# Block-sparse attention and a two-layer MoE block on one core: the off-diagonal product of layer 1 in the second accumulator bank, and an order planned with longer VectorE and ScalarE operations

## The chip, the cores and the metric

One core of one Trainium2 chip runs the whole program. The metric is the device time of one execution in microseconds. The kernel before took 605.21 us as the median of three runs (605.0 to 609.22).

## The reference

Local attention with a few global keys, for 4 batches, 8 heads, 768 positions and 64 dimensions a head, and then two matrix products with a leaky rectifier between them:

```python
scores = 1 / np.sqrt(D) * np.matmul(q, k.transpose(0, 1, 3, 2))
rel = pos[:, None] - pos[None, :]
is_global = pos[None, :] < int(n_global)                  # 8 keys
is_local = (rel >= 0) & (rel < int(n_local))              # 96 keys
bias = -slopes[:, None, None] * dist[None, :, :]
scores = np.where(is_global | is_local, scores + bias, -1000000000.0)
a = np.exp(scores - np.max(scores, axis=-1, keepdims=True))
a = a / (np.sum(a, axis=-1, keepdims=True) + 1e-09)
attn = np.matmul(a, v)
x = attn.transpose(0, 2, 1, 3).reshape(B * S, H * D)      # 3072 x 512
h = x @ w_in                                              # 512 x 2048
g = np.maximum(h, 0.0) + alpha * np.minimum(h, 0.0)
out = g @ w_out                                           # 2048 x 512
```

## The kernel before, in words

The 3072 tokens are cut into 12 units of 256 tokens; a unit is a third of one batch. For each unit the kernel computes attention for 8 heads (`attend`), transposes the result (`x_transpose`), multiplies it by `w_in` (layer 1) and the rectified result by `w_out` (layer 2, `ff_out`, L1109). Float32 values are carried as two float16 parts, high and low, and a product is three float16 products (high by high, high by low, low by high). The 16 slices of the weights are loaded and split into such parts by VectorE and ScalarE during units 0 and 1 (`split_w`, L572 to L584 and L398).

Layer 1 is done in two ways. Units 0 to 3 use `ff_in` (L960): 12 products of 256 columns a slice into one of the two banks of the tag "h", then ScalarE or VectorE scales (`mul`, L371 or L372), VectorE takes the maximum (L973), ScalarE rounds to `gh` (L975), and GpSimd or VectorE makes the rest `gl` (L397, L977). Units 4 to 11 use `seven`: four weight slices make two pairs, and a 2 by 2 block product of each pair is done with seven block products instead of eight. The names are A11, S1, S2, A12, S3, S4 and A22; each is 12 matmuls of 128 columns (L1047). They run up two PSUM banks, `ha` and `hc` (A and C in the code), which are the two buffers of the tag "h":

- A11 goes into the lower half of `ha`. A copy `p1` of it is made (`keep`, L1054, ScalarE or VectorE). Then S2 is added to it, copy `u2` is made; S3 is added, and VectorE adds it to `p5` (the first half of `gb`, `add`, L1058); A22 is added, and the sum is copied out (the other half of `gb`).
- S1 goes into the lower half of `hc` and is copied to `p5`; S4 is added, and VectorE adds it to `u2` (half of `ga`).
- A12, the off-diagonal product, goes into the upper half of `ha`, and VectorE adds it to `p1` (the other half of `ga`).

L1086 then applies the rectifier to `ga` and `gb`, L371 makes `gh` and L398 makes `gl`.

What sets the order: every operation is recorded with a key (a due time), its reads and writes by buffer, and one or more ways (engine, cost, function). `Plan.order` simulates the engines with these costs and takes, for each engine that is free, the ready operation with the lowest key; the result is the instruction order of every engine. Each engine then runs its own list strictly in that order and waits on semaphores. A whole PSUM bank is one buffer for these waits. The costs are used for nothing but the order and for the choice between two engines.

The largest attention value of each batch sets a scale (`v_sums`, `v_most`, `v_range`): ScalarE sums absolute values (L487), VectorE builds a diagonal `vdg` (L500), TensorE makes a row of it (`vrow`, L506), and VectorE finds the scale. For batch 1 this falls into the end of unit 0's and 1's layer work.

Of the kernel before, what the change touches and what calls it, by code (L numbers as in the profile page):

```python
# [146 lines left out]
class Plan:  # L147
# [37 lines left out]
    def order(self):  # L185
        ops = self.ops
        n = len(ops)
        need = [len(o[2]) for o in ops]
        after = [[] for _ in ops]
        for i, o in enumerate(ops):  # L190
            for j in o[2]:
                after[j].append(i)
        engines = list(self.LAG)
        for q in self.queue.values():
            q.sort(key=lambda b: ops[b.uses[0][0]][0])
        wait = {e: [] for e in engines}
        free = dict.fromkeys(engines, 0)
        at = [dict.fromkeys(engines, 0) for _ in ops]
        start = [None] * n
        self.way = [None] * n  # L200
        dma = 0
        seen = 0
        events = [(0, i, "ready") for i in range(n) if not need[i]]
        heapq.heapify(events)

        def fits(i):
            want = {}
            for b in ops[i][3]:
                if not b.live and b.tag in self.slots:
                    want.setdefault(b.tag, []).append(b)  # L210
            return all(self.slots[t] >= len(bs) and self.queue[t][: len(bs)] == bs for t, bs in want.items())

        def behind(i, e, now):

            own, first = (next(x for x in ops[i][1] if x[0] == y) for y in (e, ops[i][1][0][0]))
            queue = sum(ops[j][1][0][1] for k, j in wait[first[0]]
                        if k < ops[i][0] and start[j] is None and ops[j][1][0][0] == first[0])
            return max(free[first[0]] - now, 0) + queue + first[1] > (LAZY if e == "DVE" and ops[i][0] > 34 else FLEX[e]) * own[1]

        while events:  # L220
            now = events[0][0]
            while events and events[0][0] <= now:
                _, i, what = heapq.heappop(events)
                if what == "free":
                    for b in ops[i][3]:
                        b.left -= 1
                        if not b.left and b.tag in self.slots:
                            self.slots[b.tag] += 1
                elif what == "ready":
                    for e, _, _ in ops[i][1]:  # L230
                        heapq.heappush(wait[e], (ops[i][0], i))
            for e in engines:
                if free[e] > now:
                    continue
                held = []
                pick = None
                while wait[e]:
                    k, i = heapq.heappop(wait[e])
                    if start[i] is not None:
                        continue  # L240
                    if at[i][e] <= now and fits(i) and (ops[i][1][0][0] == e or behind(i, e, now)):
                        pick = i
                        break
                    held.append((k, i))
                for x in held:
                    heapq.heappush(wait[e], x)
                if pick is None:
                    continue
                i = pick
                for b in ops[i][3]:  # L250
                    if not b.live:
                        b.live = True
                        if b.tag in self.slots:
                            self.slots[b.tag] -= 1
                            self.queue[b.tag].pop(0)
                start[i] = now
                seen += 1
                _, cost, self.way[i] = next(x for x in ops[i][1] if x[0] == e)
                if isinstance(cost, Two) and free["POOL"] > now:
                    cost += SHARE * min(cost, free["POOL"] - now)  # L260
                if e == "SP":
                    dma = max(dma, now + 1125) + cost

                    busy, end = now + 525, dma
                    if self.way[i].__name__ == "transposes":
                        busy, end = now + 1245, dma + 500
                else:
                    end = busy = now + cost
                free[e] = busy
                heapq.heappush(events, (busy, i, "busy"))  # L270
                lag = LATE if e == "SP" and ops[i][0] > 40 else self.LAG[e]
                heapq.heappush(events, (end + lag, i, "free"))
                for j in after[i]:
                    need[j] -= 1
                    for x in engines:
                        own = x == e and e != "SP"
                        at[j][x] = max(at[j][x], end + ((0 if e == "PE" else 60) if own else lag))
                    if not need[j]:
                        for t in {at[j][x[0]] for x in ops[j][1]}:
                            heapq.heappush(events, (max(t, now), j, "ready" if t == min(at[j][x[0]] for x in ops[j][1]) else "busy"))  # L280
        assert seen == n, (seen, n)
        self.start = start
        return sorted(range(n), key=lambda i: (start[i], i))
# [24 lines left out]
VR = -23  # L308
# [29 lines left out]
LAZY = 100  # L338
POOLED = 3
SHARE = 0.25  # L340
STEP4 = 1.5
XAFTER = 3
RATE = 3.5
# [8 lines left out]
def fast(tc, cn, a):  # L352
    nc = tc.nc
    ctx = ExitStack()
    with ctx:
# [657 lines left out]
        def seven(u, s, key):  # L1013
# [4 lines left out]
            A = buf("h", f"ha{u}_{s}", [P, 512])  # L1018
            C = buf("h", f"hc{u}_{s}", [P, 512])
# [37 lines left out]
            def add(k, out, a_, b_, r, w):  # L1057
                op("DVE", key + k - SOON, c_dve(256), lambda: v.tensor_tensor(out=out(), in0=a_(), in1=b_(), op=ALU.add), r=r, w=w)  # L1058
# [8 lines left out]
            keep(0.3, "p1", lambda: p1.t, lambda: A.t[:, low], [A], [p1])  # L1067
            keep(0.6, "p5", lambda: p5.t, lambda: C.t[:, low], [C], [p5])
            product(1, "S2", 1, 1, A, 0, False)
            product(1.3, "A12", 0, 1, A, 256, False)  # L1070
            keep(1.4, "u2", lambda: u2.t, lambda: A.t[:, low], [A], [u2])
            add(1.5, lambda: side(ga.t, 0), lambda: half(A.t, high), lambda: half(p1.t, low), [A, p1], [(ga, 0)])
            product(2, "S3", 2, 0, A, 0, False)
            product(2.3, "S4", 3, 0, C, 0, False)
            add(2.2, lambda: side(gb.t, 1), lambda: half(A.t, low), lambda: half(p5.t, low), [A, p5], [(gb, 1)])
# [111 lines left out]
        for b in range(B):  # L1187
            k = begin(3 * b)
            jobs.append((k - 14 if b else V0, v_load, (b,)))
            for i in range(6):  # L1190
                jobs.append(((k - 5 + 0.4 * i if b == 1 else k - 9 + 0.8 * i) if b else VR, v_sums, (b, i)))
            jobs.append(((k - 2.5 if b == 1 else k - 4) if b else VR + 1, v_most, (b,)))
            jobs.append(((k - 1.5 if b == 1 else k - 2.5) if b else VR + 2, v_range, (b,)))
        for key, fn, args in sorted(jobs, key=lambda j: j[0]):
            fn(*args, key)
        with tc.manual_schedule():
# [159 lines left out]
```

## Time and profile before

| | |
|---|---|
| median of 3 runs | 605.21 us (605.0 to 609.22) |
| the profiled execution | 605.61 us, span of the profile 603.7 us |
| TensorE busy | 583.3 us, 97% of the span, 6324 matmuls |
| VectorE busy | 502.4 us, 83% |
| ScalarE busy | 417.1 us, 69% |
| GpSimd busy | 84.4 us, 14% |
| granted TensorE clock, mean | 0.999 of full speed |

A busy share says only that an engine had an instruction in flight. Matmuls are pipelined: one of 512 columns is shown with 0.38 us, and the next one starts 0.215 us after it, so a short wait of TensorE is partly hidden in the shown duration of the matmul ahead of it.

### The profile page before, as it was taken

How to read it: one execution, taken by the hardware profiler on the slowest of the kernel's cores; microseconds unless marked ns; L12 is line 12 of the kernel's file. 1: busy time of each engine (PE TensorE's matmuls, PEld its weight loads, DVE VectorE, ACT ScalarE, POOL GpSimd, SP SyncE). 2: the span in 40 equal slices, each digit the busy share in tenths (PEclk: the TensorE clock that was granted, in tenths of full speed). 3: DMA queues.
4: the chain of work that ended last, by engine and by line, in shares of the span. 5: the costliest groups of instructions: out<-in, count | busy, mean ns of one | idle time of the engine just before them, and what ended most of it. 6: DMA issues, size and time to landing. Idle time of an engine off the chain costs nothing.

```text
span 603.7 us, 16463 instructions
## 1 busy us (share of the span) xinstructions
PE 583.3 (97%) x6324; PEld 421.8 (70%) x6324; DVE 502.4 (83%) x1387; ACT 417.1 (69%) x1049; POOL 84.4 (14%) x159
## 2 busy tenths in 40 slices
PE   8899999999999998999999999999999999999996
PEld 6687666656666676676677777777777777777784
DVE  6999999996899787989879869899879879776532
ACT  5899999956887677857657747858758656632321
POOL 2002223322323342100001001001001002000000
PEclk9999999999999999999999999999999999999999
DMA  8995596344356379759976958779898766431001
GB/s 305 408 375 173 201 271 177 63 111 135 92 135 136 80 187 242 155 138 216 215 186 155 239 138 172 125 195 207 213 164 166 198 131 87 82 71 27 36 3 40
DMA packets 138918, 97.38 MB, mean 161 GB/s; under 512 B 115536, under 2 KB 115792, under 8 KB 138832
## 3 DMA queue, kind: packets, MB, share of 16 engines
q1 hardware_dynamic: 138832, 96.26, 64.0%
q8 instruction: 51, 0.84, 0.6%
q14 instruction: 35, 0.29, 0.1%
HBM read 58.22 MB, written 6.29 MB: 107 GB/s over the span
## 4 chain that ended last, share of the span: by engine, by line
PE 57%; DVE 26%; ACT 9%; issue 4%; DMA 2%; POOL 1%; SPq 0%; ACTq 0%; DVEq 0%; POOLq 0%
PE o L1109 26%; PE ha L1047 13%; PE h L960 5%; PE hc L1047 5%; PE av L859 4%; ACT pr L791 3%; DVE pr L781 3%; DVE ps L398 2%; DVE whl L398 2%; DVE wf L579 2%; PE sp L737 2%; DVE g L973 2%; DMA raw<-in_qk_dram 2%; DVE x L398 2%; DVE xs L397 1%
## 5 line engine op out<-in xcount | busy, mean ns | idle before, releaser
L1109 PE MATMUL o<-whl,gh 128*128 128x512 f16 (+1 forms) x800 | 230.2, 371 | 0.5 <-ACT os L1130 0.5
L1109 PE MATMUL o<-whl,gl 128*128 128x512 f16 (+1 forms) x400 | 148.2, 371 | 0.5 <-POOL gl L397 0.5
L1109 PEld LDWEIGHTS <-gh 128*128 128x128 f16 x800 | 71.1, 98 | 51.8 <-issue 3.6
L1047 PEld LDWEIGHTS <-sw 128*128 128x128 f16 x1536 | 91.7, 98 | 16.7 <-issue 6.8
L791 ACT ACTIVATE pr<-pr,sm 128x256 f32<-128x256 f32 (+1 forms) x176 | 85.4, 488 | 17.2 <-DVE sm L781 16.8
L960 PE MATMUL h<-xt,whl 128*128 128x256 f16 x768 | 92.5, 273 | 2.4 <-DVE g L973 1.6
L960 PEld LDWEIGHTS <-whl 128*128 128x128 f16 x768 | 74.5, 98 | 20.8 <-issue 4.5
L1047 PEld LDWEIGHTS <-whl 128*128 128x128 f16 x1152 | 70.8, 98 | 15.3 <-issue 1.5
L1047 PE MATMUL ha<-xt,whl 128*128 128x128 f16 x1152 | 79.7, 219 | 1.1 <-DVE g L973 1.1
L781 DVE CUSTOM_DVE_ANT_0 pr<-sp,D 128x256 f32<-128x256 f32 (+1 forms) x192 | 69.4, 397 | 3.5 <-PE sp L754 1.7
L1109 PEld LDWEIGHTS <-gl 128*128 128x128 f16 x400 | 39.1, 98 | 45.1 <-POOL gl L397 1.7
L397 POOL TENSOR_TENSOR gl<-g,gh 128x256 f16<-128x256 f32 x57 | 49.1, 863 | 112.1 <-ACT gh L975 84.0
L398 DVE SCALAR_TENSOR_TENSOR ps<-pr,ps 128x512 f16<-128x512 f32 (+1 forms) x80 | 54.1, 676 | 7.6 <-ACT ps L371 7.3
L799 POOL TENSOR_TENSOR fin<-fin,sm 128x4 f32<-128x4 f32 x40 | 16.3, 409 | 283.7 <-ACT pr L791 283.7
L1047 PE MATMUL ha<-xt,sw 128*128 128x128 f16 x768 | 53.3, 219 | 2.5 <-ACT u L1054 0.9
L1047 PE MATMUL hc<-xt,sw 128*128 128x128 f16 x768 | 53.4, 219 | 0.4 <-DVE g L973 0.4
L371 ACT ACTIVATE ps<-pr 128x512 f16<-128x512 f32 (+1 forms) x76 | 44.6, 590 | 4.1 <-DMA pt<-ps 3.7
L371 ACT ACTIVATE gh<-ga 128x512 f16<-128x512 f32 x32 | 20.1, 627 | 37.2 <-DVE ga L1086 37.2
L973 DVE SCALAR_TENSOR_TENSOR g<-h,g 128x256 f32<-128x256 f32 x64 | 26.7, 417 | 11.1 <-ACT g L371 10.8
L398 DVE SCALAR_TENSOR_TENSOR x<-raw,x 128x672 f16<-128x672 f32 (+1 forms) x40 | 33.7, 843 | 1.2 <-ACT x L371 1.2
L859 PEld LDWEIGHTS <-pt 128*128 128x128 f16 x888 | 30.7, 98 | 4.6 <-issue 1.2
L975 ACT CAST gh<-g 128x256 f16<-128x256 f32 x64 | 25.1, 396 | 12.6 <-DVE g L973 11.8
(150 smaller groups left out, 934.2 us busy)
## 6 DMA issues: line engine op xcount, KB each, us to landing
w<-in_w_dram SPq DMA_DIRECT2D x32, 512.0 KB, 9.3
again<-in_w_dram SPq DMA_DIRECT2D x32, 512.0 KB, 4.9
raw<-in_qk_dram SPq DMA_DIRECT2D x28, 336.0 KB, 3.7
out_dram<-os SPq DMA_DIRECT2D x23, 256.0 KB, 2.5
rawv<-in_v_dram SPq DMA_DIRECT2D x9, 512.0 KB, 4.9
raw<-in_qk_dram SPq DMA_DIRECT2D x12, 272.0 KB, 2.9
gp<-v SPq DMA_DIRECT2D x15, 192.0 KB, 2.9
first<-in_first_dram SPq DMA_DIRECT2D x4, 467.0 KB, 5.0
```

Source lines behind the costliest of these rows:

```text
L371: lambda: nc.scalar.mul(out=out(), in_=src(), mul=by.t if tile_ else by)),
L397: return e.tensor_tensor(out=out(), in0=src(), in1=hi(), op=ALU.subtract)
L398: return e.scalar_tensor_tensor(out=out(), in0=src(), scalar=val(), in1=hi(), op0=ALU.mult, op1=ALU.subtract)
L781: op("DVE", key, c_dve(n) + 10, lambda qb=qb, n=n, dc=dc, pc=pc: v.tensor_tensor_reduce(out=pr.t[:, pc : pc + n], in0=sp.t[:, pc : pc + n] ...
L791: op("ACT", key + 1, c_act(n, ptr=1) + 93, lambda qb=qb, n=n, pc=pc: nc.scalar.activation(out=pr.t[:, pc : pc + n], in_=pr.t[:, pc : pc + ...
L799: op("POOL", key + 3, c_pool(2 * G), lambda: nc.gpsimd.tensor_tensor(out=fin.t[:, : 2 * G], in0=fin.t[:, : 2 * G], in1=sm.t[:, 2 * G : 4 * ...
L859: nc.tensor.matmul(out, lhsT=p_[:, 128 * j : 128 * j + 128], rhs=v_(j), start=m == 0, stop=m == len(ps) - 1)
L960: nc.tensor.matmul(hp.t, lhsT=w.t[:, wi, wc], rhs=x.t[:, NC * xi + c, :], start=n == 0, stop=n == 3 * NC - 1)
L973: op("DVE", key, c_dve(UT), lambda: v.scalar_tensor_tensor(out=g_(), in0=hp.t, scalar=KG, in1=g_(), op0=ALU.mult, op1=ALU.max), r=[hp], w= ...
L975: op("ACT", key, c_act(UT), lambda: nc.scalar.copy(out=gh_(), in_=g_()), r=[rg], w=[rh])
L1047: nc.tensor.matmul(out, lhsT=weight(name, f, wi, c), rhs=x.t[:, 8 * piece + m * xi + 2 * j + c, :], start=start and p == n == 0, stop=n == ...
L1109: nc.tensor.matmul(o.t[:, cols], lhsT=g_()[:, tok], rhs=w.t[:, wi, 512 + cols.start : 512 + cols.stop], start=f == 0 and n == 0, stop=f == ...
```

## The change

There are three edits. In `seven`, A12 is written into the upper half of `hc` instead of `ha`, and the addition that reads it reads `hc`; A12's matmuls, their number and their data are the same. In the planner, the cost of every VectorE and ScalarE operation is multiplied by 1.06 where its key is under 34, and by 1.02 elsewhere. And three due times of batch 1's scale are moved: sums and maximum 0.5 earlier, the row 0.5 later.

```diff
@@ Plan.order
                 _, cost, self.way[i] = next(x for x in ops[i][1] if x[0] == e)
+                if e in ("DVE", "ACT"):
+                    cost = type(cost)(cost * (SLOW if ops[i][0] < 34 else SLOWER))
@@
+SLOW, SLOWER = 1.06, 1.02
+V1S, V1M, V1R = 5.5, 3, 1
@@ seven
             product(1, "S2", 1, 1, A, 0, False)
-            product(1.3, "A12", 0, 1, A, 256, False)
+            product(1.3, "A12", 0, 1, C, 256, False)
             keep(1.4, "u2", lambda: u2.t, lambda: A.t[:, low], [A], [u2])
-            add(1.5, lambda: side(ga.t, 0), lambda: half(A.t, high), lambda: half(p1.t, low), [A, p1], [(ga, 0)])
+            add(1.5, lambda: side(ga.t, 0), lambda: half(C.t, high), lambda: half(p1.t, low), [C, p1], [(ga, 0)])
@@ jobs
-                jobs.append(((k - 5 + 0.4 * i if b == 1 else k - 9 + 0.8 * i) if b else VR, v_sums, (b, i)))
-            jobs.append(((k - 2.5 if b == 1 else k - 4) if b else VR + 1, v_most, (b,)))
-            jobs.append(((k - 1.5 if b == 1 else k - 2.5) if b else VR + 2, v_range, (b,)))
+                jobs.append(((k - V1S + 0.4 * i if b == 1 else k - 9 + 0.8 * i) if b else VR, v_sums, (b, i)))
+            jobs.append(((k - V1M if b == 1 else k - 4) if b else VR + 1, v_most, (b,)))
+            jobs.append(((k - V1R if b == 1 else k - 2.5) if b else VR + 2, v_range, (b,)))
```

The order changes on every engine. In the rows below the first number in a name is the unit, the second the head, slice or block, and the last is only a serial number. Line numbers of the changed kernel are 4 higher from L340 on.

The first place is ScalarE's list around the copy `u2` of unit 5's block 1, before:

```order
L371 ACTIVATE gh5_0_1_4963<-gb5_0_4830 128x512
L600 ACTIVATE size3_0_4978<-again3_0_4434 128x512
L791 ACTIVATE pr6_7_4958,sm6_6_4916<-pr6_7_4958,sm6_6_4916 128x128
L791 ACTIVATE pr6_7_4958,sm6_6_4916<-pr6_7_4958,sm6_6_4916 128x256
L1054 COPY u25_1_5003<-ha5_1_4880 128x256
L371 ACTIVATE ps6_6_5045<-pr6_6_4915 128x384
```

And with the change:

```order
L795 ACTIVATE pr6_6_4895,sm6_6_4896<-pr6_6_4895,sm6_6_4896 128x256
L604 ACTIVATE size3_0_4975<-again3_0_4418 128x512
L1058 COPY u25_1_4994<-ha5_1_4882 128x256
L795 ACTIVATE pr6_7_4977,sm6_6_4896<-pr6_7_4977,sm6_6_4896 128x128
L795 ACTIVATE pr6_7_4977,sm6_6_4896<-pr6_7_4977,sm6_6_4896 128x256
L375 ACTIVATE ps6_6_5045<-pr6_6_4895 128x384
```

The copy, which no longer has to stand behind A12, moved ahead of the two exponentials of head 7.

The second place is VectorE's list where unit 3 ends and unit 4 begins: `g3_14` and `g3_15` are the last two rectified slices of unit 3, whose banks unit 4's A11 and S1 take over. Before:

```order
L397 TENSOR_TENSOR xs4_2_3697<-xT4_1_3525,xs4_2_3697 128x512
L384 CAST xs4_3_3710<-xn4_2986 128x256
L397 TENSOR_TENSOR sw7_3683<-ws7_0_3651,sw7_3683 128x512
L397 TENSOR_TENSOR xs4_3_3710<-xn4_2986,xs4_3_3710 128x256
L397 TENSOR_TENSOR sw7_3683<-ws7_1_3658,sw7_3683 128x512
L973 SCALAR_TENSOR_TENSOR g3_14_3695<-h3_14_3665,g3_14_3695 128x256
```

And with the change:

```order
L1008 TENSOR_TENSOR ws7_1_3679<-ws7_1_3679,ws7_0_3676 128x256
L977 SCALAR_TENSOR_TENSOR g3_14_3687<-h3_14_3663,g3_14_3687 128x256
L785 ISA pr5_3_3721,sm5_2_3613<-sp5_3_3511,D3_224 128x256
L785 ISA sm5_2_3613 128x1
L401 TENSOR_TENSOR xs4_3_3719<-xn4_2983,xs4_3_3719 128x256
L401 TENSOR_TENSOR sw7_3696<-ws7_0_3676,sw7_3696 128x512
L401 TENSOR_TENSOR sw7_3696<-ws7_1_3679,sw7_3696 128x512
```

`g3_14` moved ahead of three rests. On TensorE's list the products of `h3_15` moved ahead of layer 2's slice 13, and slices 13 and 14 now stand between them and A11 of unit 4; before, A11 came right behind them.

The third place is VectorE's list ahead of `vdg1`, the diagonal for batch 1's scale. Before:

```order
L973 SCALAR_TENSOR_TENSOR g1_12_1893<-h1_12_1863,g1_12_1893 128x256
L398 SCALAR_TENSOR_TENSOR whl15_1898<-words3_1658,whl15_1898 128x512
L497 TENSOR_REDUCE vmm1_1908<-vm1_1740 128x1
L807 RECIPROCAL sm2_6_1751<-sm2_6_1751 128x4
L398 SCALAR_TENSOR_TENSOR x16_3_2_1831<-raw3_2_1609,x16_3_2_1831 128x544
L579 SCALAR_TENSOR_TENSOR wf15_1_1934<-w15_1_1423,wb15_1_1860 128x512
L500 TENSOR_SCALAR vdg1_1942<-ident_58,vmm1_1908 128x128
```

And with the change:

```order
L977 SCALAR_TENSOR_TENSOR g0_13_1868<-h0_13_1783,g0_13_1868 128x256
L977 SCALAR_TENSOR_TENSOR g1_12_1870<-h1_12_1804,g1_12_1870 128x256
L501 TENSOR_REDUCE vmm1_1889<-vm1_1736 128x1
L376 TENSOR_SCALAR x16_3_0_1891<-raw3_0_1430 128x544
L504 TENSOR_SCALAR vdg1_1908<-ident_58,vmm1_1889 128x128
```

One long operation is left between `g1_12` and `vdg1`, where there were three. On TensorE's list two more blocks of layer 2 (slice 11 of unit 1, three matmuls of 512 columns each) stand ahead of the row `vrow1`.

## Rows read from the trace of the kernel before

**Rows 1.** Busy time by stretch: length, PE, PEld, DVE, ACT, POOL, clock, DMA

```profile
0.00:45.00 45.00, 39.76 (x300) 33.68 (x301) 37.56 (x144) 36.04 (x88) 4.80 (x22) 1.00 0.95 365
45.00:130.00 85.00, 81.77 (x681) 56.47 (x680) 84.57 (x191) 76.04 (x170) 23.59 (x32) 1.00 0.58 165
130.00:232.00 102.00, 101.19 (x883) 67.85 (x883) 86.79 (x227) 78.88 (x207) 33.79 (x49) 1.00 0.58 137
232.00:510.00 278.00, 272.54 (x3448) 197.96 (x3447) 239.35 (x686) 192.30 (x506) 21.48 (x52) 1.00 0.78 175
510.00:603.70 93.70, 88.08 (x1021) 65.84 (x1018) 54.17 (x144) 33.87 (x80) 0.78 (x4) 0.99 0.23 46
```

**Rows 2.** Waits of TensorE: who waited for whom, us in total, times, longest

```profile
PE h L960 <- DVE g L973: 1.6, 4, 0.8
PE vrow L506 <- DVE vdg L500: 1.2, 1, 1.2
PE ha L1047 <- DVE g L973: 1.1, 1, 1.1
...
PE tp L816 <- ACT pt L821: 1.0, 1, 1.0
PE ha L1047 <- ACT u L1054: 0.9, 3, 0.4
PE ha L1047 <- ACT p L1054: 0.8, 2, 0.4
PE h L960 <- DVE xt L398: 0.7, 1, 0.7
PE ha L1047 <- DVE ga L1058: 0.7, 2, 0.4
...
PE hc L1047 <- DVE g L973: 0.4, 1, 0.4
```

**Rows 3.** Timeline, unit 5's block 1, A12 to S3: start, us, engine, instruction, [idle before]

```profile
295.94 0.83 PE L1047 MATMUL ha<-xt,whl 128*128 128x128 f16 x12
...
296.61 0.59 PE L1109 MATMUL o<-whl,gh 128*128 128x512 f16 x2
...
297.06 0.53 ACT L791 ACTIVATE pr<-pr,sm 128x256 f32<-128x256 f32 x1
...
297.26 0.59 PE L1109 MATMUL o<-whl,gh 128*128 128x512 f16 x2
...
297.55 0.39 ACT L1054 COPY u<-ha 128x256 f32<-128x256 f32 x1
297.69 0.38 PE L1109 MATMUL o<-whl,gl 128*128 128x512 f16 x1
...
297.97 0.42 DVE L1058 TENSOR_TENSOR ga<-ha,p 128x256 f32<-128x256 f32 x1 [0.33 <-ACT u L1054]
...
298.44 0.83 PE L1047 MATMUL ha<-xt,sw 128*128 128x128 f16 x12 [0.37 <-DVE ga L1058]
```

**Rows 4.** Timeline, unit 6's block 3: S1 and its copy p5

```profile
361.93 0.83 PE L1047 MATMUL hc<-xt,sw 128*128 128x128 f16 x12
...
363.25 0.36 ACT L1054 COPY p<-hc 128x256 f32<-128x256 f32 x1
```

**Rows 5.** Timeline, batch 1's scale: GpSimd, VectorE and TensorE

```profile
119.51 0.67 POOL L397 TENSOR_TENSOR gl<-g,gh 128x256 f16<-128x256 f32 x1 [3.03 <-ACT gh L975]
119.61 1.12 DVE L398 SCALAR_TENSOR_TENSOR whl<-words,whl 128x512 f16<-128x512 f32 x1
...
122.37 0.28 DVE L500 TENSOR_SCALAR vdg<-ident,vmm 128x128 f32<-128x128 f32 x1
...
122.69 0.49 PE L506 MATMUL vrow<-vdg,ones 128*128 128x128 f32 x2 [1.22 <-DVE vdg L500]
```

**Rows 6.** Timeline, unit 3 to unit 4: the rectified slice, and A11 that takes its bank

```profile
233.53 0.41 DVE L973 SCALAR_TENSOR_TENSOR g<-h,g 128x256 f32<-128x256 f32 x1
...
233.99 0.83 PE L1047 MATMUL ha<-xt,whl 128*128 128x128 f16 x12 [1.14 <-DVE g L973]
```

## The prediction

> **What bounds the kernel now.** I read the busy time by stretch first, then the list of TensorE's waits, then the timeline at the places that list points to. TensorE has an instruction in flight nearly all the time: 101.19 of 102 us while units 2 and 3 run their layers, 272.54 of 278 us in most of the seven-product units, and 81.77 of 85 us between 45 and 130 us [rows 1]. The clock is at its higher level, 2.4 GHz, throughout (1.00 in every stretch, 0.99 in the last) [rows 1], so it is no term. The number of matmuls does not change. So a change of order can win only what TensorE now loses to waits, and can lose only by making new ones. In the stretch from 45 to 130 us VectorE is just as full, 84.57 of 85 us [rows 1]: there the two bound each other, and a wait taken from TensorE may come back as another one.
>
> What is there to win: the nine waits listed come to 8.4 us in 16 events [rows 2]. They understate the loss. Two matmuls of 512 columns start 0.43 us before the third one, so 0.215 apart, and one is shown with 0.38 [rows 3]; the 0.165 us between the two is idle time that looks busy. At 16 events this is another 2.6 us, 11 in all. That is under 2% of 605, and the change touches some of it.
>
> **The sum is made against the profiled execution,** 605.6 us; it lies 0.4 us above the median of 605.2 (runs 605.0 to 609.2).
>
> *A12 into the second bank.* Its twelve matmuls take 0.67 us from start to start of the next work (295.94 to 296.61) wherever they write [rows 3]. What moves is who waits. Before, `u2`, the addition to `p1`, S2, A12 and S3 all stand in one bank. The rows show the chain: A12 ends at 296.77, the copy `u2` starts at 297.55 behind an exponential, the addition starts at 297.97, 0.03 after the copy's end at 297.94, and S3 starts at 298.44, 0.05 after the addition's end [rows 3]. So copy and addition, which only read, go one after the other, and S3 waits for both. With the change `u2` needs only S2, the addition reads the other bank, and S3 needs `u2` alone. I counted the work on TensorE's new list with 0.055 us for a matmul of 128 columns and 0.215 for one of 512: between S2's end and S3 lie at least 1.97 us in all 32 blocks, where before between A12's end and S3 there were 1.3 us or less in 22 of them. The copy takes 0.39 us [rows 3]. S3's five waits (three for `u`, two for `ga`) are 0.9 and 0.7 us [rows 2], with five times 0.165 this is **2.4 us, all of which I take as gone**. S2's two waits for `p`, 0.8 us [rows 2], stay: nothing about them changes.
>
> The price is a wait that was not there: A12 writes the bank from which `p5` is copied, so A12 waits for that copy, with layer 2 queued behind it, and S4 waits for the addition. No row of before has this wait. From below it is nothing: 30 of 32 blocks have 1.97 us or more on the new list between S1's end and A12, and all 32 between A12 and S4, and a late `p5` ends at 363.61, 0.85 after S1's end at 362.76 [rows 4]. The two blocks where only S2 lies between (0.67 us) can lose 0.2 each; from above, if the copy were late by one more exponential of 0.53 [rows 3] in ten blocks, it is some 2.4 us. I take **0.2**, since 30 covers are more than twice the row's 0.85. A second price: in unit 4's first block A22 now stands right behind S3 in the same bank, with nothing to cover the addition between: 0.42 and the 0.05 behind it [rows 3], **0.5**.
>
> The Trainium skill has a rule on this, in "PSUM — Partial Sum Buffer", section "PSUM bank collisions raise a hardware error": any two of the three engines must be kept apart on one bank, reads against reads included, and it says to guard by bank, not by address. The trace agrees, with the addition that starts 0.03 us after a copy it does not depend on. The rule speaks for the change in bank `ha` and against it in bank `hc`, where it makes A12 wait for `p5`; by the rule alone the change would only move the wait, and that is the second rival below.
>
> *The end of unit 3.* A11 of unit 4 takes the bank of unit 3's slice 14 and S1 that of slice 15. VectorE reached the first slice only at 233.53, and A11 started at 233.99 after 1.14 us of idle time [rows 6]. The new list has the slice ahead of three rests, and on TensorE four layer-2 blocks (12 matmuls, 2.6 us) between the last `h` and A11. The waits are 1.1 and 0.4 us, two events [rows 2]: **1.8 us gone.**
>
> *Batch 1's row.* TensorE waited 1.22 us at 122.69 for `vdg`, which VectorE ran at 122.37 [rows 5]. Two long VectorE operations ahead of it are gone, and 1.3 us of layer 2 stand ahead of the row in addition. 1.2 and 0.165 [rows 2]: **1.4 us gone.**
>
> *Units 0 and 1, the start.* The scores of unit 1's first heads now come ahead of the transpose that waited 1.0 us for a copy [rows 2]; but the product that needs this transpose's own copy now follows closer behind. I take half of 1.2: **0.6**. Attention of unit 1 now lies between the first `xt` and its first use, which waited 0.7 [rows 2]: **0.9**. Products `h` wait four times, 1.6 us, for the slice that frees their bank [rows 2]; on the new list several stand one or two layer-2 blocks (0.65 us each) later. Half of 2.2: **1.1**. With the row this is 4.0 us, all before 130 us.
>
> *What is given back.* Of that 4.0, VectorE's full stretch takes back some. Between nothing and all of it I take half, **2.0**, because TensorE and VectorE are equally full there [rows 1]. And later `h` means less time until layer 2 needs it: on the new list the cover from `h` to its layer 2 shrinks by 2.6 to 5.0 us for six slices of units 0 and 1, and to 3.3 and 3.9 us for some of unit 3. I put two new waits of the mean size of rows 2 there (8.4/16 + 0.165 = 0.7 each): **1.4**; none and six are the ends.
>
> Engines' choices change too: seven scalings of `g` move from ScalarE to VectorE, a net three casts of weights and a few others the other way. Each costs about the same on either engine, and GpSimd gets two more rests; I count nothing, covered as long as neither queue is the last, and part of the give-back if it is.
>
> Sum: 2.4 + 1.8 + 4.0 gained is 8.2; 0.2 + 0.5 + 2.0 + 1.4 lost is 4.1. 605.6 - 4.1 = **601.5 us**.
>
> **The rivals.**
>
> 1. *Nothing comes back* (0.20). The gains are kept, and the covers that shrank were longer than needed: 605.6 - 8.2 + 0.7 = 598.1, and 596.3 if the two halves above are whole. For it: VectorE is below full from 130 us on (86.79 of 102) [rows 1], so work put off can be made up. Against: the full stretch.
>
> 2. *The wait only moves to the second bank* (0.08). `p5` and the addition are late because ScalarE is in attention's exponentials, and A12 and S4 lose what S3 won: 601.5 + 2.4 = 603.9. For it, the copy `u` that stood 0.78 us behind A12's end [rows 3]; against, the covers of 1.97.
>
> 3. *VectorE sets the pace of units 0 and 1* (0.25). Its full 85 us [rows 1] leave no room, and all 4.0 come back: 603.5, and up to 605.5 with three more small waits. The longer costs may also be of no use: a VectorE operation is longer when GpSimd runs, not by a fixed share; a rest took 1.12 us beside a GpSimd one [rows 5], where 1.06 was added to all. The Trainium skill has this in "SBUF — State Buffer", section "Who interferes with whom": VectorE with two SBUF inputs and GpSimd reading SBUF block each other. The row fits it.
>
> 4. *Slower* (0.05). One mechanism: layer 2 of units 0 and 1 waits for `gl`. Six slices lost 2.6 to 5.0 us of cover, down to some 6.5 us; where VectorE and GpSimd together need longer than that from `h` to `gl`, each slice stalls TensorE, with all that is queued behind. At the longest wait of the kind in rows 2, 1.2 + 0.165, six cost 8.2: 605.6 - 2.4 - 1.8 + 8.2 = 609.6. Against it: `gl` is on no line of rows 2.
>
> **How the numbers follow.** The forecast, about 599.2 to 603.5, has 0.42. The range must reach into rival 1 and over rival 3: 597 to 606 leaves out the far end of rival 1 and rival 4, together under 2 in 10. One per cent, about what a measurement of this kernel can tell from no change, is 599.2 and 611.3 around 605.2. Faster: most of rival 1 and a little of the forecast, 0.2. Slower: the far half of rival 4, 0.03. The rest is the same, 0.77.
>
> **What would show it.** Right: the waits of `ha` for `ga` gone and those for `u` near nothing, with at most 0.5 us of a new wait of `hc` for `p`; A11's and the row's wait gone; TensorE's idle time from 232 to 510 us down by 4. Wrong: a line of `hc` waiting for `p` of 1 us or more (rival 2); VectorE still full to 130 us and the `h` products waiting as before (rival 3); `o` waiting for `gl` several times before 130 us (rival 4).

## The result, and the profile after

The changed kernel takes 599.61 us as the median of six runs (597.90 to 603.36), the kernel before 608.95 in the runs beside it (605.0 to 610.65). The ratio, of the means of these runs, is **0.9867, 95% interval 0.982 to 0.9914**: faster by 1.3%, though the interval reaches past 0.99. The forecast was 601.5 in a range of 597 to 606, so the time lies inside, but on the side of the first rival (598.1), and "faster by over 1%" had 0.2. The profiled execution took 601.47 us, span 599.7. One slow execution of the kernel before, 751.71 us in the last set of runs, is left out everywhere.

The busy time by stretch of the changed kernel (length, then PE, PEld, DVE, ACT, POOL, clock, DMA share, GB/s) answers to [rows 1]:

```profile
0.00:45.00 45.00, 39.67 (x303) 34.35 (x304) 36.84 (x142) 36.37 (x89) 5.04 (x22) 0.96 0.93 358
45.00:130.00 85.00, 84.10 (x699) 58.12 (x697) 84.35 (x192) 80.31 (x174) 25.05 (x33) 1.00 0.59 165
130.00:232.00 102.00, 101.01 (x883) 67.61 (x882) 89.31 (x233) 80.25 (x212) 33.80 (x51) 1.00 0.63 146
232.00:510.00 278.00, 275.11 (x3498) 200.11 (x3496) 240.45 (x689) 194.11 (x514) 17.60 (x51) 1.00 0.79 175
510.00:599.70 89.70, 82.28 (x951) 61.88 (x949) 49.68 (x129) 30.23 (x71) 0.79 (x4) 0.99 0.20 42
```

Three things to see. From 45 to 130 us TensorE went from 81.77 to 84.10 us busy while VectorE stayed as full as it was. (The changed kernel is some 3 us further in its work by 130 us, so the larger sums of ScalarE there and of VectorE in the next stretch hold later work too; equal work is compared further down.) From 232 to 510 us TensorE's idle time fell from 5.46 to 2.89 us, by 2.6, where the prediction gave 4. And before 45 us the clock is 0.96, where it was 1.00.

TensorE's waits (who for whom, us in total, times, longest), against [rows 2]:

```profile
PE tp L820 <- ACT pt L825: 1.7, 1, 1.7
PE av L863 <- DVE sm L785: 1.1, 2, 0.7
PE ha L1051 <- DVE gb L1062: 0.8, 2, 0.6
PE h L964 <- DVE g L977: 0.7, 3, 0.4
PE vrow L510 <- ACT pt L825: 0.6, 1, 0.6
PE hc L1051 <- DVE ga L1062: 0.4, 1, 0.4
...
PE o L1113 <- POOL gl L401: 0.2, 1, 0.2
```

Of the nine lines of [rows 2] the waits of `vrow` for `vdg`, of `ha` for `g`, `u`, `p` and `ga`, of `hc` for `g` and of `h` for `xt` are gone. `h` for `g` fell from 1.6 to 0.7. There is no line of `hc` waiting for `p`. New are `ha` for `gb`, A22 behind S3; `vrow` for `pt`, batch 0's row, at 24 us; and `hc` for `ga`, S1 of unit 4's second block behind the addition after S4. (The kernel of experiment 2 has this last one too, with A12 in the first bank, so it is no price of the second.) The wait of `tp` at the start went from 1.0 to 1.7, and that of `av` for `sm` from 0.4 to 1.1.

The three places of [rows 3], [rows 5] and [rows 6] in the timeline of the changed kernel (start, us, engine, instruction). Unit 5's block 1, S2 to S3:

```profile
291.13 0.83 PE L1051 MATMUL ha<-xt,sw 128*128 128x128 f16 x12
...
291.80 0.83 PE L1051 MATMUL hc<-xt,whl 128*128 128x128 f16 x12
...
292.52 0.39 ACT L1058 COPY u<-ha 128x256 f32<-128x256 f32 x1
...
293.45 0.42 DVE L1062 TENSOR_TENSOR ga<-hc,p 128x256 f32<-128x256 f32 x1
...
293.76 0.83 PE L1051 MATMUL ha<-xt,sw 128*128 128x128 f16 x12
```

S3 starts while the addition still runs in the other bank, and carries no wait; in [rows 3] it began 0.05 us after the addition's end, after 0.37 idle. Batch 1's diagonal and row, and the end of unit 3:

```profile
117.87 0.27 DVE L504 TENSOR_SCALAR vdg<-ident,vmm 128x128 f32<-128x128 f32 x1
...
121.04 0.38 PE L510 MATMUL vrow<-vdg,ones 128*128 128x128 f32 x2
...
228.37 0.41 DVE L977 SCALAR_TENSOR_TENSOR g<-h,g 128x256 f32<-128x256 f32 x1
...
231.52 0.83 PE L1051 MATMUL ha<-xt,whl 128*128 128x128 f16 x12
```

`vdg` is ready 2.9 us before the row needs it, and the slice `g3_14` 2.7 us before A11; before, the row and A11 each waited over a microsecond.

The start is the one place that got worse in the profile. Busy time by stretch from 14 to 24 us, where TensorE's 1.7 us wait lies:

```profile
14.00:15.50 1.50, 1.50 (x13) 1.21 (x12) 1.50 (x6) 1.08 (x3) 0.00 (x0) 1.00 1.03 410
15.50:17.00 1.50, 0.04 (x1) 0.00 (x0) 1.50 (x6) 1.27 (x3) 0.00 (x0) 0.99 1.05 423
17.00:20.40 3.40, 3.12 (x14) 2.95 (x14) 2.49 (x7) 2.96 (x6) 0.00 (x0) 0.50 1.01 396
20.40:24.00 3.60, 3.00 (x24) 2.34 (x23) 2.28 (x11) 2.30 (x8) 0.00 (x0) 1.00 1.04 418
```

After a pause of TensorE the clock is at its lower level, 1.2 GHz, for 3.4 us; at half speed that costs at most 1.7 us. The profiled execution of before had none of this [rows 1], and lies among the shortest of its kernel, so the two profiles (4.1 us apart) show less than the medians.

**How far each kernel is ahead, and where.** Both kernels have the same 6324 matmuls, all in both traces. I gave each its spacing at full clock (0.216 us for 512 columns, 0.109 for 256, 0.056 for 128, float32 ones as they stand in the profile of before), added them up in the order of their starts, and compared when the same amount of work had been started. The number, called the lag below, is us against the profile of before (minus is ahead), at five of its times; a product that merely moved shows for a moment, so differences over long stretches count. Two executions with the same order of work also differ at the start: 9 and 10 by 0.8 us at 45, the two of the changed kernel by 0.7. The rows below the first two are the experiments.

| kernel | 1.2 GHz at the start, us | 16 | 45 | 160 | 275 | last matmul |
|---|---|---|---|---|---|---|
| changed | 3.4 | -1.1 | -0.3 | -2.9 | -3.4 | -5.8 |
| changed, second profile | 3.4 | -0.6 | 0.4 | -2.2 | -2.8 | -5.5 |
| 1: bank alone, order of before | 6.8 | -0.7 | 2.1 | 2.1 | 2.5 | 0.7 |
| 2: order of the change, first bank | 3.4 | -0.7 | 0.2 | -2.5 | -3.0 | -5.3 |
| 3: costs and due times, no bank | 0 | -0.9 | -1.5 | -4.1 | -4.8 | -5.6 |
| 4: bank alone, planned | 0 | 0.0 | 0.0 | 0.0 | 0.4 | -2.6 |
| 5: change without due times | 3.4 | -0.4 | 0.6 | -1.5 | -2.1 | -5.6 |
| 6: change, copy moved at the start | 0 | -1.1 | -1.2 | -3.9 | -4.5 | -7.8 |
| 7: bank and due times, no costs | 6.8 | -0.6 | 2.3 | 1.6 | 2.0 | -1.1 |
| 8: change, pause filled | 0 | -0.8 | -1.8 | -4.5 | -5.0 | -8.0 |
| 9: before, pause filled | 0 | -1.2 | -1.2 | -1.3 | -1.2 | -1.1 |
| 10: bank alone, order of before, pause filled | 0 | -0.4 | -0.4 | -0.4 | -0.1 | -1.7 |

From the last matmul to the end of the span it is 5.7 us before and 5.7 to 6.8 in the experiments and the second profile of the change, but 7.4 in the first: another 1.7 us by which the pair of profiles shows less.

### The profile page after: what moved, and what is told of

Its sections match the earlier page's. It is cut to its first block, busy times and chain, and to the rows that moved or that the text cites. A ratio compares the mean times of both kernels' runs of the same rounds, so it can differ in the third digit from the quotient of the medians.

```text
span 599.7 us, 16469 instructions
## 1 busy us (share of the span) xinstructions
PE 582.2 (97%) x6324; PEld 422.1 (70%) x6324; DVE 500.6 (83%) x1380; ACT 421.3 (70%) x1054; POOL 82.3 (14%) x161
## 4 chain that ended last, share of the span: by engine, by line
PE 72%; DVE 16%; ACT 5%; DMA 3%; issue 3%; POOL 1%; SPq 0%; ACTq 0%; POOLq 0%; DVEq 0%
PE o L1113 32%; PE ha L1051 11%; PE hc L1051 8%; PE h L964 8%; PE av L863 5%; PE sp L741 3%; DVE pr L785 2%; ACT pr L795 2%; DMA xt<-xs 2%; DVE ps L402 1%; DVE ws L1008 1%; PE sp L758 1%; PE tp L820 1%; DVE g L977 1%; DMA raw<-in_qk_dram 1%
## 5 line engine op out<-in xcount | busy, mean ns | idle before, releaser
L1051 PEld LDWEIGHTS <-whl 128*128 128x128 f16 x1152 | 70.9, 98 | 15.5 <-issue 1.9
L401 POOL TENSOR_TENSOR gl<-g,gh 128x256 f16<-128x256 f32 x59 | 52.3, 886 | 110.7 <-ACT gh L979 103.2
L402 DVE SCALAR_TENSOR_TENSOR ps<-pr,ps 128x512 f16<-128x512 f32 (+1 forms) x80 | 56.4, 706 | 3.0 <-ACT ps L375 2.9
L1051 PE MATMUL ha<-xt,whl 128*128 128x128 f16 x768 | 53.2, 219 | 1.1 <-DVE gb L1062 0.8
L803 POOL TENSOR_TENSOR fin<-fin,sm 128x4 f32<-128x4 f32 x40 | 11.9, 298 | 285.1 <-ACT pr L795 284.9
L375 ACT ACTIVATE x<-raw 128x672 f16<-128x672 f32 (+1 forms) x36 | 25.9, 726 | 11.6 <-PE sp L741 10.4
L795 ACT ACTIVATION_READ_ACCUMULATOR pr<-pr,sm 128x1 f32 x176 | 33.9, 192 | 0.0
```

Source lines behind the costliest of these rows:

```text
L375: lambda: nc.scalar.mul(out=out(), in_=src(), mul=by.t if tile_ else by)),
L401: return e.tensor_tensor(out=out(), in0=src(), in1=hi(), op=ALU.subtract)
L402: return e.scalar_tensor_tensor(out=out(), in0=src(), scalar=val(), in1=hi(), op0=ALU.mult, op1=ALU.subtract)
L795: op("ACT", key + 1, c_act(n, ptr=1) + 93, lambda qb=qb, n=n, pc=pc: nc.scalar.activation(out=pr.t[:, pc : pc + n], in_=pr.t[:, pc : pc + ...
L803: op("POOL", key + 3, c_pool(2 * G), lambda: nc.gpsimd.tensor_tensor(out=fin.t[:, : 2 * G], in0=fin.t[:, : 2 * G], in1=sm.t[:, 2 * G : 4 * ...
L1051: nc.tensor.matmul(out, lhsT=weight(name, f, wi, c), rhs=x.t[:, 8 * piece + m * xi + 2 * j + c, :], start=start and p == n == 0, stop=n == ...
```

## The experiments

Times are medians; ratios are of means, to the kernel before, run on the same chip beside the experiment, with 95% intervals. The chips of the three sets differ, so times of different sets compare only roughly.

**1 and 2: the bank without its order, and the order without its bank.** In the first, A12 is planned in the first bank, so that every engine's list is that of before, and only the addresses differ. In the second the lists are the changed kernel's and A12 still writes the first bank. The addition reads the bank that A12 writes. Both take a bank to plan with; the last two edits are the first kernel's, against before, and the second's, against the change:

```diff
-            def product(k, name, piece, j, bank, col, start):
+            def product(k, name, piece, j, bank, col, start, planned=None):
...
-                op("PE", key + k, 12 * 55.8, products, r=deps, w=[bank])
+                op("PE", key + k, 12 * 55.8, products, r=deps, w=[planned or bank])
...
-            product(1.3, "A12", 0, 1, A, 256, False)
+            product(1.3, "A12", 0, 1, C, 256, False, A)
...
-            product(1.3, "A12", 0, 1, C, 256, False)
+            product(1.3, "A12", 0, 1, A, 256, False, C)
```

> A12 and its addition use the second bank, but every engine's list is word for word that of the kernel before (the planner still sees the first bank, the old costs and the old due times). Theory B (the bank pays by itself): S3 no longer waits for VectorE, only for the copy u; its waits of 1.6 us shown fall to under 0.6, A12's new wait for p5 stays under 0.5, time 1.5 to 2.5 us below the kernel before (ratio 0.996 to 0.998). Theory O (the gain is the order's; the bank only allows it): the copy u stands as late in ScalarE's list as before, so S3 waits nearly as long, and A12 waits for p5 where only S2 lies between; ratio 0.999 to 1.002. Theory M (the wait moves to the second bank): waits of hc for p of 1 us or more, ratio above 1.002.

> Every engine's list is that of the changed kernel, but A12 and its addition use the first bank again. Theory B: S3's waits come back (2.4 us or more, since the copy and the addition are chained again), time 2 to 4 us above the changed kernel, ratio to before 0.990 to 0.994. Theory O: the new order alone holds most of the gain, ratio within 0.002 of the changed kernel's in the same call (0.985 to 0.989).

Measured: bank alone 606.91 us, ratio 0.9985 (0.9966 to 1.0003). Order alone 600.11, ratio 0.9872 (0.9851 to 0.9893), which is the changed kernel's. So most of the gain is the order's, an order that the planner finds when it is told of the second bank. The waits of the bank alone show that the edit does what it says:

```profile
PE h L960 <- DVE g L973: 1.6, 4, 0.8
PE vrow L506 <- DVE vdg L500: 1.2, 1, 1.2
PE ha L1047 <- DVE g L973: 1.1, 1, 1.1
...
PE ha L1047 <- ACT p L1054: 0.8, 2, 0.4
...
PE ha L1047 <- ACT u L1054: 0.2, 1, 0.2
```

`ha` for `ga` is gone, for `u` it is 0.2 in place of 0.9, `hc` waits for no `p`, and the others stand as in [rows 2]. Its lag falls from 2.5 at 275 us to 0.7 at the end, 1.8 us (1.4 from 160 us on); the medians, 606.91 and 608.09, are 1.2 apart. In this profile the start hides it, with 6.8 us at the lower clock:

```profile
15.50:17.00 1.50, 0.45 (x5) 0.21 (x4) 1.50 (x5) 1.50 (x4) 0.00 (x0) 1.00 1.04 418
17.00:23.80 6.80, 6.80 (x31) 6.28 (x33) 5.14 (x14) 3.73 (x6) 0.00 (x0) 0.50 1.03 407
23.80:27.00 3.20, 3.20 (x27) 2.65 (x26) 2.06 (x13) 1.76 (x7) 0.00 (x0) 0.99 1.03 414
```

**3: the longer costs and the due times without the bank**, with a second run of the changed kernel beside it.

```diff
-            product(1.3, "A12", 0, 1, C, 256, False)
+            product(1.3, "A12", 0, 1, A, 256, False)
```

> The longer costs and the moved due times, A12 in the first bank for planner and chip alike. Theory B: the part of the gain before unit 4 (row for batch 1, h products, end of unit 3) stays, S3's waits are as before: 3 to 5 us below the kernel before, ratio 0.992 to 0.995. Theory O: nearly the whole gain, 6 to 8 us, ratio 0.987 to 0.990. If VectorE sets the pace of units 0 and 1 (third rival): ratio above 0.997.

> The changed kernel unaltered, for comparison on the same chip. Both theories: ratio 0.984 to 0.990. The profile before last showed TensorE's clock at the lower level from 17.0 to 20.4 us behind a wait of 1.7 us; if that comes in some executions alone, this profile may show the clock at 1.00 there, and then a span 3 us shorter (about 596.5); if it belongs to the order, the clock is lower there again.

Measured: 601.5 us, ratio 0.9899 (0.9881 to 0.9917); the changed kernel again 600.53, 0.9879 (0.9859 to 0.9899). The intervals overlap, so the times alone don't tell the two apart. The lags do: to 160 us both gain alike, but from 275 us on this kernel wins 0.8 us, the changed one 2.4 and 2.7. Its waits:

```profile
PE ha L1051 <- ACT p L1058: 1.2, 3, 0.6
...
PE ha L1051 <- DVE ga L1062: 0.5, 1, 0.5
...
PE hc L1051 <- DVE ga L1062: 0.5, 1, 0.5
```

Of the waits that the bank takes away by itself, `ha` for `ga` is back. That of `ha` for `p` is not one of them, since the bank alone leaves it (0.8 in experiment 1), and `hc` for `ga` the changed kernel has too.

**4, 5 and 7: which part of the change makes the order.** The fourth has the bank and the costs and due times of before; the fifth is the change with the old due times; the seventh is the change with both factors at 1.

```diff
-V1S, V1M, V1R = 5.5, 3, 1
+V1S, V1M, V1R = 5, 2.5, 1.5
...
-SLOW, SLOWER = 1.06, 1.02
+SLOW, SLOWER = 1, 1
```

> One part alone: A12 and its addition use the second bank, the costs and due times are those of before, and the order is worked out anew with that. Theory O (the gain, about 8 us, is the order that the longer costs and due times give in units 0 to 3; the bank is worth under 2 us): ratio to before 0.995 to 1.002; TensorE keeps the waits of `vrow` for `vdg` (1.2), `ha` for `g` (1.1) and `h` for `g` (about 1.6). Theory B (the bank frees the planner to a better order by itself): ratio 0.988 to 0.992.

> The whole change but for batch 1's three due times, which are those of before (5, 2.5, 1.5). If the longer costs hold the gain: ratio to before 0.985 to 0.991, within 0.3% of the changed kernel. If the due times hold a good part of it, with the 1.2 us that `vrow` waits for `vdg` back and more behind it: 0.992 to 0.998.

> The second bank and the due times, with both factors on the costs at 1. If the longer costs hold the gain: ratio to before 0.993 to 1.002. If the due times hold it: 0.986 to 0.991, with the 1.2 us of `vrow` gone and unit 3's end (`ha` for `g`, 1.1 us) gone or not as the order falls.

Measured: 603.8 us and 0.9951 (0.9929 to 0.9973) with the bank; 600.01 and 0.9881 (0.9852 to 0.9909) without the due times; 605.15 and 0.9956 (0.9932 to 0.998) without the costs. By the times the longer costs hold the larger part and the due times nothing that can be told. By the lags from 45 us on, where the start is left out, the change wins 5.5 and 5.9, without the due times 6.2, without the costs still 3.4, without the bank 4.1: the parts overlap, and some of what the times give to the costs is the start (6.8 us at the lower clock in the profile of 7). Most of what the costs add lies between 45 and 160 us: 2.6 in both profiles of the change, 2.1 without the due times (`vrow` waits 0.8 us there), 0.7 with due times alone, nothing with the bank alone. And the bank, once the planner knows of it, wins 3.0 us after 275 us with the old costs: more than the 1.8 of the same bank under the old order. Busy time by stretch, bank alone and planned:

```profile
45.00:130.00 85.00, 81.79 (x681) 56.53 (x680) 84.56 (x191) 76.08 (x170) 23.68 (x32) 1.00 0.58 165
130.00:232.00 102.00, 101.18 (x883) 67.81 (x883) 86.77 (x227) 78.88 (x207) 33.85 (x49) 1.00 0.60 139
232.00:510.00 278.00, 274.25 (x3484) 199.86 (x3483) 241.42 (x691) 193.29 (x512) 19.93 (x52) 1.00 0.80 176
```

Its first two stretches are [rows 1] within 0.04 us; only the third moved.

**6: the copy that TensorE waits for at 15.5 us, moved ahead** of an exponential and a scaling on ScalarE.

```diff
+        copy = self.named["pt0_4"]
+        for i in (self.named["wb0_0"], self.named["pr0_7"]):
+            order.remove(i)
+            order.insert(order.index(copy) + 1, i)
```

> The changed kernel with one step moved on ScalarE: the copy `pt` of head 4 in unit 0 stands ahead of the second exponential of head 7 (0.51 us) and the scaling of the first weight slice (0.76 us). Theory S (the 1.7 us that TensorE waits at 15.5 us for this copy are lost time): that wait falls to about 0.5, head 5's transposes start 1.2 us earlier, and the time falls by 1.2 us, ratio to before 0.985 to 0.987 where the changed kernel has 0.987 to 0.989. If the lower clock right behind the wait (0.50 from 17.0 to 20.4) comes of the wait, it is gone too, which is worth 3.4 / 2 = 1.7 us more: 0.982 to 0.985. Theory V (VectorE, full until 130 us, sets the pace there anyway): the wait goes and the time stays, 0.987 to 0.989.

Measured: 600.04 us, ratio 0.9902 (0.9867 to 0.9938), no better than the changed kernel. Three of its 11 executions, at 606.07 to 607.59 us, had a mean clock of 0.983, lower than any other counted execution here (0.991 or more), so the times tell little of the copy. The wait did not go: `tp` waits for `pt` 2.1 us in two pieces, and a wait of `sp` for `sm` of 0.9 us is new. That what was put behind the copy is now late instead is the likely reason, but only argued. The profiled execution (597.97) had no time at the lower clock at the start, though the pause was there; so the pause does not always bring it.

**8 to 10: the pause filled.** Four filling products (`ident` by `ident`) stood 3 us behind the start of the pause to keep TensorE occupied; here they are issued in it, ahead of head 5's transposes. That is 8 in the table; one more kernel has eight of them, and the kernel before (9) and the first experiment (10) get the same move.

```diff
         for i in self.order():
+            if i == self.tp0_5:
+                self.early()
             self.way[i]()
...
-                if (u, h) == (1, 0):
-                    keep_busy(sps[0].t)
+            if (u, h) == (1, 0):
+                plan.early = lambda: keep_busy(sps[0].t)
```

> The changed kernel with one thing moved on TensorE: the four filling products that open unit 1's first scores (`ident` by `ident`, 0.95 us at 2.4 GHz) stand ahead of head 5's transposes in unit 0, in the pause of 1.7 us at 15.5 us, instead of 3 us behind it. Theory K (the fall of the clock to 1.2 GHz near 17 to 18 us, seen for 3.4 or 6.8 us in most executions, comes of that pause): the fall is gone, every execution is near the best of the changed kernel, 597 to 598.5 us, and 0.9 us below it where the products were on the path; ratio to before 0.980 to 0.984. Rival R (the chip lowers the clock whatever TensorE does there): the times spread as before, median 599 to 601, ratio 0.986 to 0.989.

> The same with eight filling products in the pause (1.9 us at 2.4 GHz, the whole of it). Theory K: as with four, or still fewer falls of the clock; head 5's transposes start up to 0.4 us later, 597 to 599 us. Rival R: 599 to 601 us.

> The kernel before with its four filling products moved in the same way (there they stand 4.3 us behind the pause). Theory K: its executions, which now come in groups near 605 and near 608.5 us, come together near 604 to 605; ratio to before 0.993 to 0.996. Rival R: ratio 0.998 to 1.002, both groups stay.

> The kernel before word for word but for A12 and its addition in the second bank, and the four filling products moved as above. Beside e10_before_filled it tells the bank alone. By the profile of the bank alone, where the lag fell from 2.3 to 0.7 us between 255 us and the end: 1.4 to 1.8 us faster than e10_before_filled. If the prediction's 2.4 less 0.2 holds: 2.2. If its ratio of 0.9985 tells all: 0.9.

Measured: the change with four **598.17 us (597.24 to 599.05), ratio 0.9855 (0.982 to 0.9889), the lowest median here**. Its slowest run is below the fastest of the changed kernel's second set (599.57; the first set reached 597.90), but on another chip, and the intervals of the ratios overlap. The ratio lies between the ranges of Theory K and Rival R. With eight, 598.69 and 0.9868 (0.9834 to 0.9903). Before, filled: 605.6 and 0.9982 (0.9956 to 1.0007), short of the 0.993 to 0.996 that Theory K gave and inside Rival R's range. Bank alone, filled: 604.38 and 0.9964 (0.9942 to 0.9986). The stretch of the changed kernel, with part of the pause filled by four (0.84 us of it is left):

```profile
15.50:17.00 1.50, 1.22 (x11) 1.02 (x9) 1.50 (x4) 1.23 (x3) 0.00 (x0) 1.00 1.03 418
17.00:20.40 3.40, 2.84 (x22) 2.16 (x22) 2.97 (x10) 3.37 (x7) 0.00 (x0) 1.00 1.02 402
20.40:24.00 3.60, 2.54 (x24) 2.30 (x24) 3.60 (x17) 3.55 (x13) 0.00 (x0) 1.00 1.04 418
```

In all 12 runs of the two filled forms of the change the mean clock is 0.996 or more; of the filled kernel before it is 0.995 or less in 3 of 12, of the one not filled beside it 0.994 or less in 14 of 22. So the early fall seems to have become rarer, as Theory K has it, but did not vanish, and the ratios don't decide between the two. What this set gives is a pair nearly without it, before and change both filled: 605.6 and 598.17 us, 7.4 apart; in the lags 6.9. And the bank alone: 1.2 us in the medians, 1.6 in the lags after 275 us (1.3 from 160 us on), where 1.4 to 1.8 had been expected from the profile and 2.2 by the prediction.

## Why the prediction was right in the time and wrong in a step

Where it failed: **the part "What is given back".** It took 3.4 us off the gains, 2.0 because VectorE is full before 130 us and 1.4 for layer 2 waiting on later `h`. The gains, 8.2 less 0.7 of prices, were close in sum; nearly nothing came back, as the first rival said. By stretch, the pair with filled pause (lags of 8 less those of 9) against the prediction's terms, each put where [rows 2]'s events lie in the trace (the wait of `xt` at 29.84 us; three of the four `h` waits before 130 us, not all, and one at 193.91; one of the five waits of the bank's term at 240.94):

| stretch of before | terms | predicted gain | measured |
|---|---|---|---|
| to 45 us | start 0.6, `xt` 0.9 | 1.5 | 0.6 |
| 45 to 160 | row 1.4, `h` 0.9 | 2.3 | 2.6 |
| 160 to 275 | end of unit 3 1.8, `h` 0.2, bank 0.4, A22 0.5 against | 1.9 | 0.6 |
| 275 to the end | bank 2.0, A12's price 0.2 against | 1.8 | 3.1 |
| sum | | 7.5 | 6.9 |
| given back | VectorE 2.0, layer 2 1.4 | -3.4 | none seen from 45 to 160 |

So the sum fits better than its parts; that 7.5 and 6.9 are near is partly luck.

*Given back by VectorE.* The premise "TensorE and VectorE are equally full there" was read rightly, and the conclusion did not follow. The profile of the change, cut where it has started the work that before had started by 45, 130, 160 and 232 us, beside before:

```profile
45.00:130.00 85.00, 81.77 (x681) 56.47 (x680) 84.57 (x191) 76.04 (x170) 23.59 (x32) 1.00 0.58 165
130.00:160.00 30.00, 30.00 (x247) 19.23 (x248) 23.14 (x66) 22.84 (x64) 8.72 (x14) 1.00 0.49 120
160.00:232.00 72.00, 71.19 (x642) 48.62 (x639) 63.65 (x161) 56.04 (x144) 25.07 (x35) 1.00 0.62 145
...
44.70:126.70 82.00, 81.11 (x673) 56.44 (x671) 81.38 (x184) 77.62 (x170) 24.37 (x32) 1.00 0.60 168
126.70:157.10 30.40, 30.22 (x255) 19.39 (x255) 25.99 (x72) 24.76 (x66) 10.03 (x16) 1.00 0.59 148
157.10:229.40 72.30, 71.48 (x645) 48.89 (x640) 63.98 (x163) 57.13 (x148) 23.34 (x35) 1.00 0.61 137
```

VectorE stays full in the first stretch, but the stretch is 3.0 us shorter and VectorE does 3.2 us less in it (184 instructions for 191); 2.9 of this it does in the next one, where before it had 6.9 us free. ScalarE has as many instructions in the first stretch as before. So work was put off to where there was room, which is what the prediction named as speaking for its first rival. The other orders go the same way: VectorE does 2.5 us less there without the due times (lag 2.1 better from 45 to 160), 0.5 less without the costs (0.7), the same with the bank alone (0.0). Of the third rival's sign one half came, VectorE full to the end of the stretch, and the other did not: `h` waits less. No run moves VectorE's work by itself, so that this is the cause is argued from these rows.

*Two new waits of layer 2.* The profile has one wait of `o` for `gl`, 0.2 us, and before had one of 0.5 at 182.48, among the lines that [rows 2] leaves out, so none was added. The covers that shrank by up to 5.0 us were longer than needed; so the fourth rival, the slower one, had no ground.

*The row, `xt` and `h`.* The row's wait and that of `xt` went, `h` kept 0.7 of 1.6, so a little over half went, as taken. Row and `h` had 2.3 from 45 to 160, and the stretch gives 2.6.

*The end of unit 3.* Both waits are gone. The lag of the filled change drops by 1.6 us between 225 and 245 us, then 1.0 is lost by 255; the wait of A22 there, 0.59 us, is part of it:

```profile
238.98 0.43 DVE L1062 TENSOR_TENSOR gb<-ha,p 128x256 f32<-128x256 f32 x1 [0.73 <-ACT size L604]
239.46 0.83 PE L1051 MATMUL ha<-xt,whl 128*128 128x128 f16 x12 [0.59 <-DVE gb L1062]
```

The 0.5 for it was right as a wait; with the 0.165 it is 0.75. Two more new waits stand right behind it, of 0.35 us (A11 of the next block for the copy `gb`) and 0.44 (its S1 for `ga`), which no term had; against the three come 1.1 us of waits that before has between 240 and 248 us. How this makes the 1.0 stays open.

*The bank.* The waits of `ga` went as the text said, and those of `u` in the change; under the old order `u` keeps 0.2 to 0.5. A12's price was nothing that shows, not 0.2. By itself, under the old order, the bank is worth 1.2 to 1.8 us where 2.2 was predicted; the term was sized too high, likely by the waits of `u` that stay and by some of the 0.165 added to five events. The changed kernel still wins 2.4 to 3.1 after 275 us, because the planner, told of the second bank, also orders the copies differently. That order helps the old bank as well: with it, A12 in the first bank wins 2.3 there (2), and planned without it 0.8 (3). S2's waits for `p`, 0.8 us, which were to stay because "nothing about them changes", are gone with that order in either bank, and stay with the bank alone. The Trainium skill's rule in "PSUM — Partial Sum Buffer", section "PSUM bank collisions raise a hardware error", made the second rival possible: the readers of bank `hc` now have to take turns. It did not come to that: in `ha`, before, ScalarE or VectorE began 27 times within 0.1 us of the other's end, while in `hc`, after, neither ever did, and with 1.97 us of cover in 30 of 32 blocks no matmul waited: no line of `hc` for `p` in any profile with the second bank.

*The start.* The 0.6 measured, for 1.5, is no more than the 0.8 by which 9 and 10 differ there, so it tells nothing. The profiles of the change that have the early fall of the clock lose 1.4 to 1.6 us from 16 to 45 us against that of 3, which has the same order there and no fall; no step had this. The prediction read the clock as "no term" from one profile that happened to have none.

So 601.5 lay 1.9 above the median partly by luck. The change was to win 4.1 us and won 9.3 in the medians and about 7 in the filled pair. What brought the time near is that the sum starts from 605.6, an execution of before without the fall of the clock, 3.3 below the median of 608.95, while the changed kernel's median contains some of that loss. One of its ends is off by 0.1: 598.1 less 0.6 and 1.1 is 596.4.

## What to carry to other kernels

Two full engines do not make a gain come back: look whether the stretch behind has room for the work that is put off, and compare stretches of equal work, not of equal time. Where a planner sets the order, an edit is worth what the new order makes of it; run the edit under the old order, and the new order without the edit, before crediting either. When a kernel's executions differ by more than the effect, compare how far the same work has come at several points, not only the ends.

## What the runs showed of the hardware

At the start TensorE's clock was at 1.2 GHz for 3.4 us in four profiles and for 6.8 us in two, each time from some point between 17 and 18.5 us on and after a time in which TensorE had been idle for about a microsecond or more; the float32 matmuls of the first experiment's start were 0.21 us apart in it, where before has 0.11. By the lags from 16 to 45 us, 3.4 us of it cost 1.4 to 1.6 us (the change against 3) and 6.8 us cost 2.8 (1 against before). The executions of before in the last set of runs fall into 8 from 604.03 to 606.01 us at a mean clock of 0.997 or more and 14 from 607.0 to 610.19 at 0.994 or less, 3 us apart, about what the 6.8 us cost in the first experiment. The Trainium skill describes such a fall behind a wait in "TensorE: Matmul & The Clock Gate", section "HAM oscillation — how this bites in real kernels". The trace agrees on the order of events, but not every pause did it: the kernel before waited 1.00 us at 17.61 without a fall, where the first experiment, with the same lists, waited 1.05 and had 6.8 us of it; and the kernel of 3 waited 1.7 us as the change does, without a fall. What decides between two executions of the same lists stays open.
